# Staging keys and queries in two full PSUM banks, the last query chunk's maxima from one block-diagonal operand, and a fourth split step per head

## The chip, the cores and the metric

The kernel runs on one core of a Trainium2 chip. TensorE (PE in the rows; its weight loads are PEld) multiplies matrices into PSUM, VectorE (DVE) and ScalarE (ACT) read PSUM and write on-chip memory, GpSimd (POOL) works on on-chip memory alone, and SyncE (SP) issues the DMAs. Each engine runs its own instructions in order. The metric is device time per execution in microseconds (us), the median of several executions. Before the change it is 1091.69 us (three runs, 1090.48 to 1095.55).

## What is computed

Three layers follow each other, all in float32. The first is attention over 4 batches of 8 heads, with 576 queries (each the mean of two rows of q) and 1152 keys of 64 elements:

```
q_pool = q.reshape(B, H, S // 2, 2, D).mean(axis=3)
scores = scale * q_pool @ k^T
attn   = softmax(scores);  out = attn @ v
```

The second is a mixture of four causal attention heads over 576 tokens of 512 features, of which two per token count. The third mixes each token with the one before it, and multiplies a sigmoid gate with the product of a squared ReLU layer of 1024 and a second matrix.

## The kernel before

A float32 number goes through TensorE in one of two ways. Either a matmul takes the float32 operand as it is ("native", line 786; a native matmul is two records in the trace), or the number is split into a rounded high part and the rest, both of a faster type, and products of the parts are summed: high by high, high by low, low by high (lines 793 to 795). A copy with rounding makes the high part, a subtraction the low part (`dve_lo`, line 145).

The first layer runs head after head, 32 of them (`hh`), each in nine steps (`s1_job`). A step takes two 128-key chunks of one half of the queries (288 of them). It makes two tiles of scores with two matmuls each: KA by QA (line 758) and KB by QB (line 759). KA holds the keys' high parts twice (in partitions 0 to 63 and 64 to 127), QA the queries' high and low parts; KB holds the keys' low parts and a row of ones, QB the queries' high parts and, in row 64, the negative maximum of each query, so that the exponential (ACT, line 766) needs nothing more. A step then is `n` (native: the exponentials p multiply the float32 values in VF) or `sv` (ACT copies the high part ph, line 64, and DVE subtracts, line 71, giving pl). In heads 2 to 31, steps 0, 3 and 6 are native, the other six are split. The product with the values follows four steps later.

Beside the steps runs the work for later heads, as tasks that are spread over a stretch of steps:

- `s1_prep(hh+2)`, from three steps before the start of head `hh` to one step after it. POOL adds the pairs of query rows; TensorE transposes the keys (line 635, four transposes into one PSUM bank, a fifth into a second) and the queries (line 681, three into a third bank). The keys are copied and subtracted into a staging tile `sk` (high and low), of which there is one buffer; the copies are ACT's in batch 0 and DVE's after it (`kh0`, `kh1`). The queries go straight from PSUM into QA (two copies by ACT, two subtractions by DVE, each 64 by 288). Two steps later in the program, SP issues six DMAs from `sk` to KA and KB (lines 670 to 672) and two from QA to QB (line 711).
- `s1_max(hh+1)`, from 4.5 steps before the start of head `hh` to at least 4.5 steps after it (somewhat later in heads 0 to 2): for each of five query chunks (four of 128, the last of 64) three matmuls of 384 keys (line 728), each with a DVE maximum over the 384 (line 730). `max_finish` turns the result by a transpose (line 402), and one DMA writes the row of QB (line 404).

In batches 1 to 3 the second layer's work of the batch before is merged between the steps of heads 0 to 6 (queries and keys, line 348; its attention, lines 467 to 496; its output, line 548). Heads 2 to 8, 15 and 23 have none of it: nine plain steps.

All instructions of the first two layers are written in program order and then placed on the engines by a scheduler; TensorE is the exception, whose order is the written one. Four PSUM banks ("bank") serve transposes, maxima and sums of values alike, two pairs of banks ("st") the scores.

Of the kernel before, what the change touches and what calls it, by code (L numbers as in the profile page):

```python
# [55 lines left out]
def tile_kernel(ctx: ExitStack, tc: tile.TileContext, q, k, v, w_gate, wq, wk, wv, wo,  # L56
# [112 lines left out]
    def drive(steps, tasks, drain=False):  # L169
# [4 lines left out]
        for i, st in enumerate(steps):  # L174
# [219 lines left out]
    def max_finish(PMs, QB, name):  # L394
# [176 lines left out]
    EK = -(-NC // 2) * P  # L571
# [16 lines left out]
    raw = {}  # L588
# [23 lines left out]
    def s1_prep(hh):  # L612
# [16 lines left out]
        def tk(c0, c1):  # L629
            def f():  # L630
# [6 lines left out]
                e0 = c0 // 2 * P  # L637
                if kst:
                    hi, lo_ = (sk[:m, j, e0 : e0 + w] for j in range(2))
                    copy(kh, hi, ps[:m, :w])  # L640
                    dve_lo(lo_, ps[:m, :w], hi)
                else:
                    for up in range(m // D):
                        a, cs = own[up], slice(e0 + up * EK, e0 + up * EK + w)
                        copy(kh, KAi[a, cs], ps[a, :w])
                        if first:
                            act_hi(KAi[own[1 - up], cs], ps[a, :w])
                    for up in range(m // D):
                        a, cs = own[up], slice(e0 + up * EK, e0 + up * EK + w)
                        los.append((KBi[0:D, cs], ps[a, :w], KAi[a, cs]))  # L650
                    if not first:
                        lo()
                if c1 == NC and not first:
                    later(G["dup"], dup_k)
# [7 lines left out]

        halves = (slice(0, EK), slice(EK, S))

        def dup_k():
            for up in range(2):
                a, z, cs = own[up], own[1 - up], halves[up]
                w = cs.stop - cs.start
                if kst:
                    nc.sync.dma_start(f32(KAi[a, cs]), f32(sk[a, 0, :w]))  # L670
                    nc.sync.dma_start(f32(KAi[z, cs]), f32(sk[a, 0, :w]))
                    nc.sync.dma_start(f32(KBi[0:D, cs]), f32(sk[a, 1, :w]))
                else:
                    nc.sync.dma_start(f32(KAi[z, cs]), f32(KAi[a, cs]))
# [3 lines left out]
        def tq():  # L678
            ps = aux()
            for t in range(NQ // 2):  # L680
                nc.tensor.transpose(ps[:, t * QW : (t + 1) * QW], qp[:, 2 * t * D : (2 * t + 2) * D], ident[:QW, :QW])  # L681
            qq.append(ps)
            if qst:
                copy(G["qh" + ("0" if hh < H else "1")], sq[:, 0], ps[:, :HT])
                dve_lo(sq[:, 1], ps[:, :HT], sq[:, 0])
            else:
# [617 lines left out]
```

## Time and profile before

| | |
|---|---|
| median of 3 runs | 1091.69 us |
| profiled execution | 1094.68 us, of which the span of the core's instructions is 1092.3 us |
| mean granted TensorE clock | 0.986 of full |
| TensorE busy | 1024.0 us (94%) |
| TensorE weight loads | 884.7 us (81%) |
| DVE busy | 826.6 us (76%) |
| ACT busy | 583.8 us (53%) |

The profiled execution took 3.0 us more than the median. The heads of the first layer fill the span from 7.5 us to about 739 us (first and last matmul of line 758). Busy times overlap: a matmul's record lasts 0.29 us while the next one starts 0.13 us after it, so a busy share of TensorE is more than the share in which columns flow.

### The profile page before, as it was taken

To read this page: it belongs to the slowest core of one execution; us is meant where nothing else is said; L and a number is where in the kernel's file an instruction comes from. 1 tells how busy PE (TensorE), PEld (TensorE's weight loads), DVE (VectorE), ACT (ScalarE), POOL (GpSimd) and SP (SyncE) were. 2 spreads that over 40 slices of the span, in tenths; PEclk is the share of its full clock that TensorE was granted. 3 is DMA by queue.
4 is the path that set the end of the run, shared out by engine and by line. 5 is a ranking of instruction groups with operands and counts; after the bars stand their busy time and mean duration, and the time that the engine had idled before them with its cause. 6 is when DMAs were issued, how large, how long until landed. Compare 5 with 4: busy or idle time off the path is not lost. (4 is left out here: it accounts for less than half of the span.)

```text
span 1092.3 us, 18217 instructions
## 1 busy us (share of the span) xinstructions
PE 1024.0 (94%) x6480; PEld 884.7 (81%) x6480; DVE 826.6 (76%) x1753; ACT 583.8 (53%) x1011; POOL 187.8 (17%) x277
## 2 busy tenths in 40 slices
PE   5999999998999999999999999988888799999998
PEld 3888888887887887787788888878876688888887
DVE  5899999789899889799989988876776634444442
ACT  4667777557576556666656666663454312222222
POOL 6341111011111102021201111021012001111110
PEclk9999999999999999999999999999898899999999
DMA  5656545344543544544454453147245311111100
GB/s 123 147 136 158 128 117 141 101 116 111 132 132 93 161 117 116 147 124 113 107 170 127 98 140 85 38 148 233 98 163 154 112 44 39 40 39 39 39 21 19
DMA packets 129095, 119.23 MB, mean 109 GB/s; under 512 B 63751, under 2 KB 91358, under 8 KB 129006
## 3 DMA queue, kind: packets, MB, share of 16 engines
q1 hardware_dynamic: 129006, 118.08, 40.4%
q8 instruction: 51, 0.84, 0.3%
q14 instruction: 38, 0.31, 0.1%
HBM read 63.24 MB, written 20.07 MB: 76 GB/s over the span
## 5 line engine op out<-in xcount | busy, mean ns | idle before, releaser
L730 DVE TENSOR_REDUCE PM<-bank 128x1 f32<-128x384 f32 (+1 forms) x480 | 254.3, 546 | 27.3 <-PE bank L728 23.6
L766 ACT ACTIVATE p<-st 128x576 f32<-128x576 f32 x288 | 186.4, 649 | 117.0 <-PE st L759 113.2
L728 PE MATMUL bank<-KA,QA 128*128 128x384 f32 (+1 forms) x480 | 187.0, 398 | 15.6 <-DVE KB L145 4.3
L758 PE MATMUL st<-QA,KA 128*128 128x288 f32 x576 | 176.7, 320 | 3.4 <-ACT p L766 2.9
L759 PE MATMUL st<-QB,KB 65*128 65x288 f32 x576 | 163.9, 299 | 0.0
L71 DVE TENSOR_TENSOR pl<-p,ph 128x576 fp32r<-128x576 f32 x190 | 148.3, 781 | 13.1 <-ACT ph L64 11.1
L64 ACT ACTIVATE ph<-p 128x576 fp32r<-128x576 f32 x190 | 130.2, 685 | 17.1 <-PE bank L794 7.3
L758 PEld LDWEIGHTS st<-QA,KA 128*128 128x128 f32 x576 | 110.5, 192 | 13.3 <-ACT p L766 4.0
L793 PE MATMUL bank<-ph,VV 128*65 128x288 f32 x384 | 117.5, 306 | 1.9 <-DVE sk L145 0.9
L728 PEld LDWEIGHTS bank<-KA,QA 128*128 128x128 f32 (+1 forms) x480 | 87.9, 185 | 36.4 <-DVE PM L730 8.1
L786 PE MATMUL bank<-p,VF 128*65 128x288 f32 x384 | 114.6, 409 | 0.7 <-DVE PM L409 0.6
L795 PE MATMUL bank<-pl,VV 128*65 128x288 f32 x384 | 113.2, 295 | 0.0
L794 PE MATMUL bank<-ph,VV 128*64 128x288 f32 x384 | 112.9, 294 | 0.0
L759 PEld LDWEIGHTS st<-QB,KB 65*128 65x128 f32 x576 | 110.5, 192 | 2.4
L1101 PE MATMUL sth<-xkh,wk 128*128 128x256 f32 x512 | 91.4, 279 | 1.2 <-ACT relu L1108 1.2
L1108 ACT ACTIVATE relu<-sth 128x512 f32<-128x512 f32 x32 | 17.5, 596 | 122.4 <-PE sth L1101 121.6
L1101 PEld LDWEIGHTS sth<-xkh,wk 128*128 128x128 f32 x512 | 78.7, 188 | 1.8 <-ACT relu L1108 1.4
L71 POOL TENSOR_TENSOR VV<-VF,VV 128x576 fp32r<-128x576 f32 x32 | 44.7, 1396 | 200.2 <-ACT VV L64 175.0
L625 POOL TENSOR_TENSOR qp<-qr 96x384 f32<-96x384 f32 x31 | 34.5, 1113 | 217.1 <-PE bank L681 162.7
L1101 PE MATMUL sth<-xkl,wk 128*128 128x256 f32 x256 | 71.4, 279 | 0.0
L786 PEld LDWEIGHTS bank<-p,VF 128*65 128x65 f32 x384 | 51.9, 139 | 20.4 <-DVE PM L409 1.2
L482 POOL TENSOR_SCALAR_AFFINE_SELECT p<-p 128x128 f32<-128x128 f32 (+1 forms) x96 | 34.4, 388 | 196.5 <-ACT p L474 196.4
(205 smaller groups left out, 2235.5 us busy)
## 6 DMA issues: line engine op xcount, KB each, us to landing
KA<-sk SPq DMA_DIRECT2D x60, 160.0 KB
qr<-in_q_dram SPq DMA_DIRECT2D x32, 288.0 KB
kr<-in_k_dram SPq DMA_DIRECT2D x32, 288.0 KB
VF<-in_v_dram SPq DMA_DIRECT2D x32, 288.0 KB
KA<-sk SPq DMA_DIRECT2D x60, 128.0 KB
R<-scr SPq DMA_DIRECT2D x48, 144.0 KB
w3h<-w3st SPq DMA_DIRECT2D x20, 256.0 KB
w3l<-w3st SPq DMA_DIRECT2D x20, 256.0 KB
```

Source lines behind the costliest of these rows:

```text
L64: nc.scalar.activation(dst, src, AF.Copy)
L71: eng[e].tensor_tensor(dst, src, hi.bitcast(F32), op=ALU.subtract)
L728: nc.tensor.matmul(ps[:n, : 3 * P], QA[i][:, t0 : t0 + n], KA[i][:, 3 * g * P : 3 * (g + 1) * P], start=True, stop=True)
L730: nc.vector.tensor_reduce(pm[:n, c, g : g + 1], ps[:n, : 3 * P], axis=AX.X, op=ALU.max)
L758: nc.tensor.matmul(st[:, n, :HT], KA[i][:, ks], QA[i][:, cs], start=True, stop=False)
L759: nc.tensor.matmul(st[:, n, :HT], KB[i][0 : D + 1, ks], QB[i][0 : D + 1, cs], start=False, stop=True)
L766: nc.scalar.activation(pt, st[:, :, :HT], AF.Exp, scale=1.0 / 16.0)
L786: nc.tensor.matmul(a[: D + 1, :HT], VF[hh % NF][:, c], cell["p"][:, n], start=c == 0, stop=c == NC - 1)
L793: nc.tensor.matmul(a[: D + 1, :HT], vh, ph[:, n], start=c == 0, stop=False)
L794: nc.tensor.matmul(a[:D, :HT], vl, ph[:, n], start=False, stop=False)
L795: nc.tensor.matmul(a[: D + 1, :HT], vh, pl[:, n], start=False, stop=c == NC - 1)
L1101: nc.tensor.matmul(st[:, f // 2, f % 2 * GT : (f % 2 + 1) * GT], w[kt][:, fs], x[:, kt], start=i == 0, stop=i == 3 * KT - 1)
```

## The change

1. **Split steps.** In heads 2 to 31 step 3 turns from native into split; two native steps (0 and 6) are left.
2. **Staging.** The tile `sk` becomes wider (640 key columns and 288 query columns, high and low). The first bank of keys is staged as before. A second bank takes one more transpose of the keys (the last two chunks together) and the three transposes of the queries, and one copy and one subtraction of 416 columns on all 128 partitions move it into `sk`. So the fifth key transpose's own copy and subtraction and the four 64 by 288 operations on the queries go. The copies are ACT's in all heads (`kh1` is `s`). QA and QB are now filled from `sk` by six DMAs, where two were. The order of the key columns in KA changes with the layout (`kcol`).
3. **Maxima of the last 64 queries.** Two DMAs write the last 64 queries' high parts into a block-diagonal operand `BD`: partitions 0 to 63 with columns 0 to 63, partitions 64 to 127 with columns 64 to 127. One matmul of BD with the 512 first columns of `sk` gives the scores of these queries against the even chunks in rows 0 to 63 and against the odd chunks in rows 64 to 127; a second one with 128 columns gives chunk 8 (and chunk 7 once more). Two maxima (512 and 128 columns) stand where three of 384 stood. A small minimum joins the two halves of the row (negative maxima), and the row of QB is written by two DMAs.
4. **TensorE's order at the start.** The first steps of head 0, up to three before head 1, are driven outside the manual order, so that the scheduler places TensorE's instructions there too.

The core of the diff; of the table G, which is one line, only the two entries for the split steps and one for the copies differ:

```diff
-'S0': ('n', 'sv', 'sv', 'n', 'sv', 'sv', 'n', 'sv', 'sv')
+'S0': ('n', 'sv', 'sv', 'sv', 'sv', 'sv', 'n', 'sv', 'sv')
-'S1': ('n', 'sv', 'sv', 'n', 'sv', 'sv', 'n', 'sv', 'sv')
+'S1': ('n', 'sv', 'sv', 'sv', 'sv', 'sv', 'n', 'sv', 'sv')
-'kh1': 'v'
+'kh1': 's'
...
-            nc.sync.dma_start(f32(QB[D : D + 1, 0 : 5 * P]).rearrange("o (a c) -> o a c", a=5), f32(mr))
+            if not halves:
+                nc.sync.dma_start(f32(QB[D : D + 1, 0 : 5 * P]).rearrange("o (a c) -> o a c", a=5), f32(mr))
+                return
+            n = T % P
+            low = sm.tile([5, n], F32R, tag="ml", name=f"ml{name}")
+            nc.vector.tensor_tensor(low, f32(mr[:, :n]), f32(mr[:, n:]), op=ALU.min)
+            nc.sync.dma_start(f32(QB[D : D + 1, 0 : 4 * P]).rearrange("o (a c) -> o a c", a=4), f32(mr[0:4]))
+            nc.sync.dma_start(f32(QB[D : D + 1, 4 * P : T]), f32(low[4:5]))
...
-    EK = -(-NC // 2) * P
+    EK = NC // 2 * P
+    SW = EK + P
...
+        sk = None if first else s1a.tile([P, 2, SW + HT], F32R, tag="sk", name=f"sk{hh}")
...
+        def stage(ps, c, w):
+            copy(kh, sk[:, 0, c : c + w], ps[:, :w])
+            dve_lo(sk[:, 1, c : c + w], ps[:, :w], sk[:, 0, c : c + w])
...
+        def tkq():
+            ps = aux()
+            qq.append(ps)
+            nc.tensor.transpose(ps[:, :P], kr[:, (NC - 2) * D : NC * D], ident)
+            tq(P)
+            stage(ps, EK, P + HT)
+            later(G["dup"], dup_q)
+            later(G["dup"], dup_k)
...
-                    nc.sync.dma_start(f32(QBi[0:D, cs]), f32(QAi[a, cs]))
+                nc.sync.dma_start(f32(QAi[a, cs]), f32(sk[a, 0, SW:]))
+                nc.sync.dma_start(f32(QAi[z, cs]), f32(sk[a, 1, SW:]))
+                nc.sync.dma_start(f32(QBi[0:D, cs]), f32(sk[a, 0, SW:]))
+            n = T % P
+            for up in range(2):
+                nc.sync.dma_start(f32(BD[hh % 2][own[up], up * D : up * D + n]), f32(sk[own[1], 0, SW + HT - n :]))
...
+        def half(g):
+            c0, w = ((0, EK), (EK, P))[g]
+
+            def f():
+                if hh < 4 and g == 0:
+                    nc.vector.memset(pm[:, len(TC) - 1, 2:3], -3.0e38)
+                ps = aux()
+                nc.tensor.matmul(ps[:, :w], BD[hh % 2], staged[hh][:, 0, c0 : c0 + w], start=True, stop=True)
+                nc.vector.tensor_reduce(pm[:, len(TC) - 1, g : g + 1], ps[:, :w], axis=AX.X, op=ALU.max)
+            return f
+
+        if hh >= G["nf1"]:
+            return [half(0), half(1)] + some(0, len(TC) - 1) + [lambda: max_finish(pm, QB[i], f"1_{hh}", True)]
...
+    free = at_[1][0] - 3
+    drive(steps[:free], tasks)
     with tc.manual_schedule(engines={mybir.EngineType.PE}):
-        drive(steps, tasks, drain=True)
+        drive(steps[free:], tasks, drain=True, first=free)
```

How the instructions stand, at three places. The first is TensorE around the start of head 6, a head of plain steps: the staging transposes of head 8 and the first maximum of head 8. In the names, `st_6_0` is the score tile of head 6, step 0; `kr` and `qp` are the raw keys and pooled queries; `p` and `ph` the exponentials. Before:

```order
L635 MATMUL bank_1773<-ident,kr_1602 64x128
...
L758 MATMUL st_6_0_1789<-QA_177,KA_175 128x288
L759 MATMUL st_6_0_1789<-QB_178,KB_176 128x288
...
L728 MATMUL bank_1797<-KA_179,QA_181 128x384
L681 MATMUL bank_1800<-ident,qp_1725 128x96 x3
...
L759 MATMUL st_6_4_1898<-QB_178,KB_176 128x288
L786 MATMUL bank_1910<-p_6_0_1794,VF_185 65x288
L728 MATMUL bank_1912<-KA_171,QA_173 128x384
```

And in the changed kernel:

```order
L735 MATMUL bank_1826<-KA_179,QA_181 128x384
L699 MATMUL bank_1829<-ident,kr_1632 128x128
L685 MATMUL bank_1829<-ident,qp_1765 128x96 x3
L778 MATMUL st_6_0_1836<-QA_177,KA_175 128x288
L779 MATMUL st_6_0_1836<-QB_178,KB_176 128x288
...
L779 MATMUL st_6_4_1943<-QB_178,KB_176 128x288
L806 MATMUL bank_1955<-p_6_0_1841,VF_185 65x288
L750 MATMUL bank_1957<-sk_1766,BD_198 128x512
```

The query transposes moved from behind the scores of step 0 to ahead of them, into the bank of the last key transpose, and the first maximum of head 8 (line 750), at the same place as before, now reads `sk` and BD in the place of KA and QA. Between the staging transposes and that maximum lie five steps' scores, six maxima of 384 columns, 18 matmuls of split steps and three native ones (of two records each).

The second place is SP's queue for the same staging of head 8 (`sk_1726` before, `sk_1766` in the changed kernel). Before:

```order
L255 DMA R_4_1661<-scr_4_1660 64x576
L670 DMA KA_171<-sk_1726 64x512
L597 DMA kr_1834<-in_k_dram 128x576
L671 DMA KA_171<-sk_1726 64x512
L670 DMA KA_171<-sk_1726 64x640
L671 DMA KA_171<-sk_1726 64x640
L672 DMA KB_172<-sk_1726 64x640
L672 DMA KB_172<-sk_1726 64x512
L711 DMA QB_174<-QA_173 64x288 x2
L602 DMA VF_186<-in_v_dram 128x9x64
```

And in the changed kernel (the left-out rows are the same three of the second half of the queries, and the rest of the keys):

```order
L675 DMA KA_171<-sk_1766 64x512
L255 DMA R_4_1697<-scr_4_1696 64x576
L612 DMA kr_1873<-in_k_dram 128x576
L715 DMA QA_173<-sk_1766 64x288
L716 DMA QA_173<-sk_1766 64x288
L717 DMA QB_174<-sk_1766 64x288
...
L720 DMA BD_198<-sk_1766 64x64 x2
L676 DMA KA_171<-sk_1766 64x512
L677 DMA KB_172<-sk_1766 64x512
...
L617 DMA VF_186<-in_v_dram 128x9x64
```

Ahead of BD's two DMAs stand six for the queries, of which the second (line 716) reads the low part; five of the six DMAs for the keys come behind BD.

The third place is the start: SP's rows from the keys of head 2 to the row of maxima of head 1 (`mr_1`). Before:

```order
L672 DMA KB_172<-sk_366 64x640
L597 DMA kr_489<-in_k_dram 128x576
L711 DMA QB_174<-QA_173 64x288 x2
L596 DMA qr_657<-in_q_dram 96x6x128
L404 DMA QB_182<-mr_1_499 1x5x128
```

And in the changed kernel:

```order
L716 DMA QA_173<-sk_368 64x288
...
L720 DMA BD_198<-sk_368 64x64 x2
L677 DMA KB_172<-sk_368 64x512
L675 DMA KA_171<-sk_368 64x640
L676 DMA KA_171<-sk_368 64x640
L677 DMA KB_172<-sk_368 64x640
L405 DMA QB_182<-mr_1_502 1x5x128
```

The row for head 1 (line 405) stands behind all of head 2's staging DMAs, ten of them from the first that reads the queries' low part.

## Rows read from the trace of the kernel before

**Rows 1.** The page's busy times: us, share of the span, instructions.

```profile
PE 1024.0 (94%) x6480; PEld 884.7 (81%) x6480; DVE 826.6 (76%) x1753; ACT 583.8 (53%) x1011; POOL 187.8 (17%) x277
```

**Rows 2.** Busy times by stretch: us from the start, its length, each engine, granted clock.

```profile
core 0: us, PE busy (x) PEld busy (x) DVE busy (x) ACT busy (x) POOL busy (x), PEclk, DMA share, GB/s
61.00:181.00 120.00, 116.31 (x758) 100.19 (x756) 113.44 (x224) 87.98 (x151) 22.36 (x20) 1.00 0.57 137
255.00:338.00 83.00, 77.28 (x499) 66.10 (x498) 74.12 (x170) 52.23 (x91) 13.69 (x22) 0.98 0.44 115
331.00:335.00 4.00, 4.00 (x18) 3.74 (x19) 3.13 (x7) 1.58 (x3) 0.78 (x3) 0.60 0.02 5
454.00:537.00 83.00, 77.22 (x501) 66.00 (x500) 74.42 (x170) 53.56 (x94) 13.85 (x23) 0.98 0.43 112
631.00:724.00 93.00, 91.69 (x610) 79.30 (x609) 75.80 (x175) 62.36 (x108) 11.73 (x21) 1.00 0.36 86
```

**Rows 3.** TensorE's timeline in head 0: start, us, line, output and inputs.

```profile
39.76 1.13 PE L786 MATMUL bank<-p,VF 128*65 128x288 f32 x4
40.52 0.51 PE L758 MATMUL st<-QA,KA 128*128 128x288 f32 x1
...
41.26 0.34 PE L728 MATMUL bank<-KA,QA 128*128 128x384 f32 x1
41.44 0.29 PE L793 MATMUL bank<-ph,VV 128*65 128x288 f32 x1
41.57 0.29 PE L794 MATMUL bank<-ph,VV 128*64 128x288 f32 x1
```

**Rows 4.** Groups by shape: count, busy us, mean ns, idle before and its releaser.

```profile
L71 DVE TENSOR_TENSOR pl<-p,ph 128x576 fp32r<-128x576 f32 x190 | 148.3, 781 | 13.1 <-ACT ph L64 11.1 <-PE st L759 0.6
L64 ACT ACTIVATE ph<-p 128x576 fp32r<-128x576 f32 x190 | 130.2, 685 | 17.1 <-PE bank L794 7.3 <-ACT U L134 3.1 <-DVE sk L66 1.1
...
L730 DVE TENSOR_REDUCE PM<-bank 64x1 f32<-64x384 f32 x96 | 51.1, 540 | 6.1 <-PE bank L728 5.5
...
L145 DVE TENSOR_TENSOR QA<-bank,QA 64x288 fp32r<-64x288 f32 x64 | 29.1, 454 | 5.9 <-ACT QA L64 4.6
...
L64 ACT ACTIVATE QA<-bank 64x288 fp32r<-64x288 f32 x63 | 25.3, 402 | 5.3 <-PE bank L681 4.4
...
L145 DVE TENSOR_TENSOR sk<-bank,sk 128x512 fp32r<-128x512 f32 x30 | 20.4, 681 | 0.4 <-ACT sk L64 0.3
...
L66 DVE CAST sk<-bank 128x512 fp32r<-128x512 f32 x24 | 16.3, 678 | 0.5 <-PE bank L635 0.5
```

**Rows 5.** Instructions on the staging tile: count, duration ns least/median/most, first and last start.

```profile
L145 DVE TENSOR_TENSOR sk<-bank,sk x60: 269/477/692, 31.0 to 676.9; 128x512 fp32r<-128x512 f32 x30, 64x128 fp32r<-64x128 f32 x30
...
L672 SPq DMA_DIRECT2D KB<-sk x60: 461/554/1587, 32.2 to 680.3; - x60
...
L64 ACT ACTIVATE sk<-bank x12: 254/420/599, 30.4 to 113.7; 128x512 fp32r<-128x512 f32 x6, 64x128 fp32r<-64x128 f32 x6
```

**Rows 6.** The same view of the tile of maxima: a maximum over 512 columns.

```profile
L428 DVE TENSOR_REDUCE PM<-bank x16: 667/672/678, 221.6 to 816.0; 64x1 f32<-64x512 f32 x16
```

**Rows 7.** Waits of TensorE, 61 to 724 us: total us, times, longest.

```profile
PE bank L728 <- DVE PM L730: 3.2, 7, 1.2
```

**Rows 8.** SP's timeline around the start of head 6: start, us.

```profile
127.34 0.50 SPq L251 DMA_DIRECT2D scr<-rd  x1
129.04 0.47 SPq L255 DMA_DIRECT2D R<-scr  x1
...
134.79 1.57 SPq L711 DMA_DIRECT2D QB<-QA  x2
```

**Rows 9.** TensorE's timeline in head 5: the query transposes of head 7.

```profile
115.10 0.41 PE L681 MATMUL bank<-ident,qp 96*128 96x96 f32 x3
```

**Rows 10.** DVE's timeline there: the low parts of the same queries.

```profile
117.28 0.92 DVE L145 TENSOR_TENSOR QA<-bank,QA 64x288 fp32r<-64x288 f32 x2
```

**Rows 11.** SP's timeline at the start: the row of maxima of head 1.

```profile
38.40 0.85 SPq L404 DMA_DIRECT2D QB<-mr  x1
```

**Rows 12.** TensorE's timeline: the first scores of head 1.

```profile
43.46 0.30 PE L758 MATMUL st<-QA,KA 128*128 128x288 f32 x1
```

More of the change, by code (lines that the diff above doesn't have):

```diff
@@ L167, in tile_kernel, with drive @@
     lagged = []
-    def drive(steps, tasks, drain=False):
+    def drive(steps, tasks, drain=False, first=0):
         def fill(t):
@@ L172, in fill @@
                 x.run(t)
-        for i, st in enumerate(steps):
+        for i, st in enumerate(steps, first):
             now[0] += 1
@@ L586, in tile_kernel, with kcol @@
         nc.vector.memset(PM[i], 0.0)
-    raw = {}
+    BD = [s1.tile([P, P], F32R, name=f"BD{i}") for i in range(2)]
+    for i in range(2):
+        nc.gpsimd.memset(f32(BD[i]), 0.0)
+    raw, staged = {}, {}
+    def kcol(c):
+        return 2 * EK if c == NC - 1 else c // 2 * P + c % 2 * EK
     def s1_load(hh):
@@ L616, in s1_prep @@
         own = (slice(0, D), slice(D, P))
-        kst, qst = (G["kst"] and not first, G["qst"] and not first)
         KAi, KBi, QAi, QBi = KA[i], KB[i], QA[i], QB[i]
         qp = s1a.tile([QW, NQ * D], F32, tag="qp", name=f"qp{hh}")
-        sk = s1a.tile([P, 2, EK], F32R, tag="sk", name=f"sk{hh}") if kst else None
-        sq = s1a.tile([P, 2, HT], F32R, tag="sq", name=f"sq{hh}") if qst else None
+        sk = None if first else s1a.tile([P, 2, SW + HT], F32R, tag="sk", name=f"sk{hh}")
+        staged[hh] = sk
         kh = G["kh" + ("0" if hh < H else "1")] if hh else "s"
@@ L636, in f @@
                     w += P
[L637 to L654, printed above, removed]
+                if not first:
+                    stage(ps, 0, w)
+                    return
+                cols = [(own[up], own[1 - up], slice(kcol(c0 + up), kcol(c0 + up) + w)) for up in range(m // D)]
+                for a, z, cs in cols:
+                    copy(kh, KAi[a, cs], ps[a, :w])
+                    act_hi(KAi[z, cs], ps[a, :w])
+                for a, z, cs in cols:
+                    los.append((KBi[0:D, cs], ps[a, :w], KAi[a, cs]))
             return f
@@ L676, in s1_prep, with tq @@
-        qhalf = (slice(0, HT), slice(HT, T))
-        def tq():
+            for up, cs in enumerate((slice(0, EK), slice(EK, S))):
+                a, z, w = own[up], own[1 - up], cs.stop - cs.start
+                nc.sync.dma_start(f32(KAi[a, cs]), f32(sk[a, 0, :w]))
+                nc.sync.dma_start(f32(KAi[z, cs]), f32(sk[a, 0, :w]))
+                nc.sync.dma_start(f32(KBi[0:D, cs]), f32(sk[a, 1, :w]))
+        qhalf = (slice(0, HT), slice(HT, T))
+        def tq(w0=0):
+            ps = qq[-1] if w0 else aux()
+            for t in range(NQ // 2):
+                c = w0 + t * QW
+                nc.tensor.transpose(ps[:, c : c + QW], qp[:, 2 * t * D : (2 * t + 2) * D], ident[:QW, :QW])
+            if w0:
+                return
+            qq.append(ps)
+            for up in range(2):
+                a, cs = own[up], qhalf[up]
+                copy(G["qh" + ("0" if hh < H else "1")] if hh else "sv"[up], QAi[a, cs], ps[a, :HT])
+            for up in range(2):
+                a, z, cs = own[up], own[1 - up], qhalf[up]
+                dve_lo(QAi[z, cs], ps[a, :HT], QAi[a, cs])
@@ L679, in tq @@
+        def tkq():
             ps = aux()
-            for t in range(NQ // 2):
-                nc.tensor.transpose(ps[:, t * QW : (t + 1) * QW], qp[:, 2 * t * D : (2 * t + 2) * D], ident[:QW, :QW])
             qq.append(ps)
[L683 to L686, printed above, removed]
-                for up in range(2):
-                    a, cs = own[up], qhalf[up]
-                    copy(G["qh" + ("0" if hh < H else "1")] if hh else "sv"[up], QAi[a, cs], ps[a, :HT])
-                for up in range(2):
-                    a, z, cs = own[up], own[1 - up], qhalf[up]
-                    dve_lo(QAi[z, cs], ps[a, :HT], QAi[a, cs])
@@ L693, in tq @@
-            if not first:
-                later(G["dup"], dup_q)
+            nc.tensor.transpose(ps[:, :P], kr[:, (NC - 2) * D : NC * D], ident)
[3 more added lines that the diff above has]
+            later(G["dup"], dup_k)
         qq = []
@@ L755, in qk @@
                 for n, (j, c) in enumerate(items):
[L756 removed]
+                    cs, k0 = slice(j * HT, (j + 1) * HT), kcol(c)
                     ks = slice(k0, k0 + P)
```

24 lines of the change are left out of this document (4 added, 20 removed).

## The prediction, made before the changed kernel ran

> **What bounds the kernel now.** I read the busy times of the page first [rows 1]: TensorE stands at 94% and DVE at 76%, ACT at 53%. An average over unlike heads doesn't say which of the two ends a head, so I cut the span by heads next [rows 2]. The reader is to see three kinds. The 120 us from 61 are seven plain heads of 17.1 us each: TensorE 116.3, DVE 113.4 (95%). The two stretches of 83 us are three heads each (12 to 14, 20 to 22) with much of the second layer: TensorE 93%, DVE 89 to 90%, clock 0.98. I count 11 such heavy heads (10, 12 to 14, 17, 18, 20 to 22, 25, 26). The 93 us from 631 (heads 27 to 30) stand for the ten others, light for DVE: TensorE 98.6%, DVE 82%. So in light heads TensorE alone sets the time; in plain ones both are nearly full; in heavy ones TensorE has gaps while DVE is close to full.
>
> The timeline of TensorE [rows 3] says what a busy share is worth: split matmuls of 288 columns last 0.29 us but start 0.13 apart (41.44, 41.57), a maximum of 384 holds the next one back by 0.18 (41.26 to 41.44). So the columns need less than the record's time, and the gaps inside are real, though small.
>
> **TensorE's part.** A native step has two products, four records from 39.76. The next matmul begins at 40.52 and lasts 0.51 where one of its size lasts 0.29, so its columns flow from 40.74: 0.98 us for two products, 0.49 each [rows 3]. A split product is three matmuls of 0.13, 0.39. The change turns two per head: 2 x 0.10 = 0.20 us less. A chunk's three maxima are 3 x 0.18 = 0.54; instead come 512 columns (0.18 x 512/384 = 0.24) and 128 (0.06 by columns, 0.13 if it goes like one of 288; I take 0.10): 0.20 less. The transposes are as many as before. Together 0.40 us per head, 12 us in 30 heads.
>
> **DVE's part** [rows 4 to 6]. Per head there go three maxima of 384 on the last chunk (3 x 0.540), two low parts of the queries (2 x 0.454) and the low part of 128 keys (0.28; the 60 low parts of `sk` lie at 0.269 to 0.692, half of them that small): 2.81. In the 24 heads of batches 1 to 3 the two copies, 0.678 and about 0.27, go as well: 3.76. There come one pl (0.781), a low part of 416 columns (between 0.454 at 288 and 0.681 at 512; 0.58), a maximum of 512 (0.672), one of 128 (0.28, as for the small low part) and a small minimum (0 to 0.27; 0.20): 2.51. Net 0.30 less in 6 heads, 1.25 less in 24: 31.8 us.
>
> ACT pays for it: in batches 1 to 3 one ph (0.685), a copy of 512 (0.42 to 0.60) and of 416 (about 0.51) come, two of 0.402 go: +1.0 per head, some 25 us in all. In heavy heads ACT is busy 52 to 54 of 83 us [rows 2], so that hides; were it late, the score tiles would come free later, at most its 1.0 per head.
>
> **What a microsecond of DVE is worth.** In heavy heads I take 1.1 of 1.25 us: DVE reads the banks that TensorE waits for, and the stretch has 5.7 us without TensorE records in 83, 1.9 per head. But the waits named for that in 660 us are small: three maxima account for 3.2 us in 7 waits, at most 1.2 [rows 7]. So the low end is TensorE's own 0.40, the high one 1.25. 11 x 1.1 = 12.1 us (4 to 14). In light heads TensorE's 0.40 counts: 4.0 us (0 to 12, if DVE's part counts there too).
>
> The Trainium skill, page "Perfetto Trace Analysis", section "Identifying the Most-Contended Engine", holds that matmul busy time judges TensorE badly, that its weight-load share is the better measure, and that the engine with the highest occupancy is the one to improve first. By that DVE, 113.4 against 100.2 us of weight loads in the plain heads and 74.1 against 66.1 in the heavy ones [rows 2], would be the bound, and its whole cut would be the gain: rival B below. The trace agrees in so far as records overlap (0.29 against 0.13), and disagrees in the light heads, where DVE has 17 us idle in 93.
>
> **The new chain to BD.** The maxima of head hh+2's last chunk used to read KA and QA; now they need `sk` and BD, and BD comes by DMA behind six others on SP. In a plain head the staging transposes and the first of these maxima stand where they stood, with this between them: 20 score matmuls (2.6 us), six maxima (1.08), 18 split matmuls (2.36), three native products (1.47): 7.5 us. The chain: landing of a DMA takes some 1.7 us (the row of scr at 127.34, the one that reads it at 129.04), an issue 0.55 us in the median, 0.79 in a pair, 1.59 at worst [rows 5, 8]. From the end of the query transposes (115.10 + 0.41) to their low parts (117.28) pass 1.8 us, plus 0.58 for the new one: 2.35 [rows 9, 10]. Then, counting from the first issue that needs the low part, six issues to the second BD: 6 x 0.554 = 3.3, or 6 x 0.79 = 4.7; then 1.7. That is 7.4 to 8.75 us against 7.5, and 6.2 if the low part comes at once. BD is late by 0 to 1.3 us; I take 0.3. What queues behind that matmul on TensorE is everything: the scores of the next steps, hence ACT and DVE. Plain heads: 9 x (-0.40 + 0.3) = -0.9 us (-3.6 to +9). In heavy and light heads the second layer's matmuls widen the 7.5 us, and I put the wait at nothing. The six of `sk`'s DMAs that the next head's copies wait for have a whole head's time. SP issues seven more DMAs per head, 4 us of 17: hidden otherwise.
>
> **Start.** Head 1's row of maxima was issued at 38.40 and head 1's scores began at 43.46 [rows 11, 12]. It now stands behind ten DMAs after head 2's low part: 10 x 0.55 = 5.5 us, of which part was there before (eight then), and with the landing and the row's own issue I get 43.6 to 46.2 for the scores, against 43.46. The first steps of head 0, which the scheduler may now place between tasks, can lose or gain about as much. I take +2.5 (-2 to +6).
>
> **Clock.** At 331 to 335 the granted clock is 0.60 in the mean, so for most of it the lower level of 1.2 GHz; 0.98 over each 83 us is 1.7 us lost each [rows 2]. TensorE had idled before it. With a shorter DVE some such dips go: -2 us (-5, all of them and two alike, to +3, new ones behind BD).
>
> **Sum** against the profiled execution, 1094.68: -12.1 - 4.0 - 0.9 + 2.5 - 2 = -16.5, 1078.2. The runs' median is 3.0 lower: 1075 us, 1.5% less.
>
> **Rivals.**
> A is the forecast, 1075, by its terms' bounds 1066 to 1086: chance 0.55.
> B: DVE sets the pace everywhere, since each PSUM bank comes free only when DVE has read it. For it: 95% and 89% in plain and heavy heads. Against: the light heads, and the small named waits. Then all 31.8 us go: 1060. Chance 0.13.
> C: nothing much comes. In heavy heads the banks turn by the latency from engine to engine, not by DVE's load, so only 0.40 x 11 = 4 us go; light heads 2, plain heads +2, start +4, clock 0: 1092. For it: the small waits of [rows 7]; against: DVE at 89%, where a later arrival queues. Chance 0.18.
> D, slower: the queue of SP. If the issues that follow the low part take 1.0 us each (between the median 0.55 and the worst 1.59), BD comes at 2.35 + 6.0 + 1.7 = 10.0 us, 2.5 late, in nine plain heads: +22.5, start +4.5; against it -12.1 - 4.0 - 3.6. That is +7.3: 1099. It cancels the gain from 1.7 us of wait per plain head on, and is slower by over 0.5% from 2.3. For it: five of seven issues new and in one row; against: the median. Chance 0.14.
> That the change doesn't do what it says I exclude: the order shows both maxima on BD, and the split steps.
>
> **How the numbers follow.** A measurement of this kernel can tell about 0.5%, 5.5 us, from no change, so below 1086.2 is faster and above 1097.2 slower. Faster: 0.52 of A, all of B, 0.03 of C: 0.68. Same: 0.03 of A, 0.14 of C, 0.03 of D: 0.20. Slower: 0.01 of C, 0.11 of D: 0.12. The range goes from B's 1060 to 1094, so that half of B and most of D, under 0.2, are outside. A's own range is 1066 to 1086.
>
> **What would show it.** DVE's busy time near 795 us, ACT's near 609. Heavy stretches shorter by 3 x 1.1 us, light ones by 0.4 per head, plain ones by nearly nothing. Waits of TensorE on a DMA into BD of at most 0.3 us per plain head (2.5 would be D). Head 1's first scores near 46 us. Clock above 0.98 in the heavy stretches. I am wrong if DVE's share falls in heavy heads and their length doesn't (C), or if light and plain heads shrink by over 1 us each (B).

## The result, and the profile of the changed kernel

The changed kernel takes 1103.71 us (median of five runs, 1101.27 to 1111.82); the kernel before has a median of 1094.2 us over five runs, the three earlier ones included. The ratio, which weighs all the runs and not the medians alone (their quotient is 1.0087), is 1.0107, 95% interval 1.0062 to 1.0152: 1.1% slower, where 1.5% faster was forecast. The profiled execution, 1111.82 us, is the slowest of the five. It is 17 us longer than the profiled one of the kernel before, where the medians differ by 9.5, so its waits and its low clock stand for somewhat more than the median's loss.

The page's busy times, which answer to [rows 1]:

```profile
PE 1021.6 (92%) x6510; PEld 895.8 (81%) x6510; DVE 803.3 (72%) x1677; ACT 597.1 (54%) x1029; POOL 189.2 (17%) x279
```

DVE lost work as intended, and its share fell with no gain. So I cut the span as before, by heads, now from the first exponential of a head. Heads 0 and 1, heads 2 to 31, the plain heads 5 to 7, the heavy ones 12 to 14 and the light ones 27 to 30, changed kernel (columns as in [rows 2]):

```profile
18.90:69.30 50.40, 41.23 (x219) 33.57 (x218) 34.42 (x74) 26.90 (x49) 15.77 (x17) 0.86 0.49 112
69.30:751.90 682.60, 639.78 (x4287) 566.14 (x4285) 570.45 (x1225) 451.34 (x784) 109.84 (x144) 0.98 0.56 136
125.40:177.80 52.40, 48.71 (x328) 43.18 (x327) 44.68 (x88) 38.16 (x66) 6.90 (x6) 1.00 0.62 138
266.30:349.20 82.90, 75.90 (x499) 65.34 (x498) 72.66 (x164) 54.72 (x96) 12.03 (x23) 0.98 0.54 136
647.30:741.60 94.30, 91.70 (x626) 80.88 (x624) 75.85 (x172) 64.57 (x111) 16.37 (x28) 1.00 0.44 105
```

The same cuts in the kernel before:

```profile
62.30:739.20 676.90, 646.85 (x4259) 559.81 (x4258) 595.21 (x1303) 436.95 (x763) 106.45 (x142) 0.99 0.48 123
115.10:166.00 50.90, 49.63 (x326) 42.94 (x325) 49.06 (x98) 36.92 (x63) 7.23 (x6) 1.00 0.53 129
255.80:338.50 82.70, 76.98 (x496) 65.64 (x494) 74.34 (x171) 51.57 (x91) 14.19 (x23) 0.98 0.45 116
631.40:728.70 97.30, 93.78 (x625) 81.14 (x623) 77.91 (x177) 63.30 (x109) 14.91 (x28) 1.00 0.39 99
19.00:62.30 43.30, 38.17 (x219) 31.43 (x219) 35.18 (x76) 27.66 (x54) 17.59 (x19) 1.00 0.51 123
```

Length less TensorE's busy time is the time without a matmul. In heads 2 to 31 that was 676.9 - 646.9 = 30.0 us and is now 682.6 - 639.8 = 42.8. TensorE has 7 us less to do, and waits 13 more. Of these stretches only the light one got shorter (94.3 for 97.3); the plain one went from 50.9 to 52.4, with DVE down from 96% to 85%. Cut head by head in the same way, the eleven heavy heads took 3.3 us more in all, the nine plain ones 2.9 more and the ten light ones 0.5 less; heads 16, 21 and 24 alone took 4 to 5 us more each. The first two heads took 7.1 us more. What follows the first layer is untouched by the change; it took 358 us in this execution, 353 in the one of before.

Part of what remains is a slower clock. These are five of the seven stretches at the lower level (0.50, 1.2 GHz) in the changed kernel's first layer:

```profile
96.40:99.80 3.40, 3.35 (x12) 2.56 (x13) 1.47 (x4) 0.41 (x1) 0.00 (x0) 0.50 0.93 202
28.10:34.90 6.80, 6.27 (x20) 4.93 (x20) 5.88 (x13) 3.71 (x7) 2.84 (x4) 0.50 0.42 106
45.20:52.00 6.80, 6.23 (x24) 4.64 (x23) 3.44 (x7) 1.93 (x3) 0.00 (x0) 0.50 0.75 167
372.90:379.70 6.80, 6.56 (x25) 6.03 (x26) 2.07 (x3) 0.88 (x3) 0.00 (x0) 0.50 0.66 159
512.80:519.60 6.80, 6.63 (x30) 6.23 (x30) 3.96 (x10) 1.72 (x3) 0.70 (x3) 0.50 0.17 61
```

At half speed they cost 30.6 / 2 = 15.3 us; with the other two, of 3.4 us each (at 321.7 and 574.3), it is 18.7 us. In its first layer the kernel before had three such stretches of 3.4 us (one in [rows 2]), 5.1 us lost. In the changed kernel TensorE had stood still for 1.3 to 3.7 us shortly before each of them. Its longest totals of waits from 60 to 760 us, changed kernel:

```profile
PE st L476 <- DMA QB<-mr: 6.3, 5, 2.1
PE sto L556 <- ACT YH L64: 6.0, 2, 3.4
PE bank L750 <- DMA BD<-sk: 4.5, 2, 3.7
```

(YH is the high part of the second layer's normalised output; line 476 multiplies its scores, line 556 its output.)

The longest, 3.7 us, is in head 3. Three engines around it (a timeline: start, us; in brackets the idle time before and its releaser), first POOL:

```profile
88.48 1.29 POOL L148 TENSOR_TENSOR wo_l<-wst,wo_h 128x512 fp32r<-128x512 f32 x1
```

then SP:

```profile
86.09 0.53 SPq L612 DMA_DIRECT2D kr<-in_k_dram  x1
89.80 0.33 SPq L876 DMA_DIRECT2D wst<-in_moe_wo_dram  x1
90.22 0.48 SPq L715 DMA_DIRECT2D QA<-sk  x1
...
93.94 1.23 SPq L720 DMA_DIRECT2D BD<-sk  x2
```

and TensorE:

```profile
92.12 0.65 PE L806 MATMUL bank<-p,VF 128*65 128x288 f32 x2
96.45 0.76 PE L750 MATMUL bank<-sk,BD 128*128 128x512 f32 x1 [3.68 <-DMA BD<-sk]
```

The next weights (line 876) go into a tile with one buffer. SP stood at that DMA from 86.62 until POOL had read the old ones at 89.77; then six DMAs of the queries and two of BD followed, the last at 95.17, and TensorE waited until 96.45.

Head 21 shows the other kind: a row of maxima of the second layer. DVE finishes it (`mr`) at 508.07, and SP issues two other DMAs first:

```profile
507.80 0.27 DVE L403 CAST mr<-bank 5x128 fp32r<-5x128 f32 x1
508.23 0.52 SPq L245 DMA_DIRECT2D sd<-U  x1
508.85 0.52 SPq L611 DMA_DIRECT2D qr<-in_q_dram  x1
509.81 0.77 SPq L405 DMA_DIRECT2D QB<-mr  x1
...
512.97 0.58 PE L476 MATMUL st<-QB,KB 65*128 65x288 f32 x1 [2.08 <-DMA QB<-mr]
```

The same row in the kernel before:

```profile
496.72 0.27 DVE L403 CAST mr<-bank 5x128 fp32r<-5x128 f32 x1
497.02 0.76 SPq L404 DMA_DIRECT2D QB<-mr  x1
```

It was issued at once; now it starts 1.7 us after its data, TensorE waits 2.08 us, and the clock is at its lower level from 512.8 to 519.6.

The plain heads show a third kind, and here it is DVE that waits. TensorE waited for BD only once in heads 5 to 7, for 0.8 us. But the sums that normalise a head's output go through three small DMAs on SP (`sd<-U`, `scr<-rd`, `R<-scr`), and DVE stands once per head until `R` is there. Its waits for it in heads 5 to 7, then the rows of heads 5 and 6 (ACT, SP, POOL, DVE):

```profile
DVE XT L835 <- DMA R<-scr: 3.9, 3, 1.8
```

```profile
133.25 0.48 ACT L134 ACTIVATE U<-bank,epsc 65x288 f32<-65x288 f32 x1
134.91 0.53 SPq L245 DMA_DIRECT2D sd<-U  x1
140.95 0.55 SPq L255 DMA_DIRECT2D R<-scr  x1
144.62 1.33 POOL L71 TENSOR_TENSOR VV<-VF,VV 128x576 fp32r<-128x576 f32 x1
145.28 1.28 DVE L835 TENSOR_TENSOR XT<-U,R 64x576 f32<-64x576 f32 x1 [0.93 <-DMA R<-scr]
```

The sums are written at 133.73. SP has issued staging DMAs one after another since 125.94, twelve of them, and comes to the first small one at 134.91, 1.2 us late (0.03 in the kernel before, at 123.35). The product with `R` then falls beside a subtraction of POOL's and takes 1.28 us (1.28 to 1.48 in the three heads, 0.75 in the kernel before). In the kernel before DVE had no such wait in these heads.

### The profile page after: what moved, and what is told of

Read it like the earlier page. It is cut to its first block, busy times and chain, and to the rows that moved or that the text cites. A ratio compares the mean times of both kernels' runs of the same rounds, so it can differ in the third digit from the quotient of the medians.

```text
span 1110.0 us, 18515 instructions
## 1 busy us (share of the span) xinstructions
PE 1021.6 (92%) x6510; PEld 895.8 (81%) x6510; DVE 803.3 (72%) x1677; ACT 597.1 (54%) x1029; POOL 189.2 (17%) x279
## 5 line engine op out<-in xcount | busy, mean ns | idle before, releaser
L737 DVE TENSOR_REDUCE PM<-bank 128x1 f32<-128x384 f32 (+1 forms) x390 | 208.0, 547 | 40.3 <-PE bank L735 38.1
L71 DVE TENSOR_TENSOR pl<-p,ph 128x576 fp32r<-128x576 f32 x220 | 171.5, 780 | 13.4 <-ACT ph L64 11.7
L64 ACT ACTIVATE ph<-p 128x576 fp32r<-128x576 f32 x220 | 150.1, 683 | 33.0 <-PE bank L814 23.7
L735 PE MATMUL bank<-KA,QA 128*128 128x384 f32 (+1 forms) x390 | 152.3, 402 | 12.8 <-DVE KB L145 4.4
L813 PE MATMUL bank<-ph,VV 128*65 128x288 f32 x444 | 134.1, 302 | 1.2 <-DVE sk L145 1.0
L815 PE MATMUL bank<-pl,VV 128*65 128x288 f32 x444 | 132.1, 298 | 0.6 <-DVE pl L71 0.6
L814 PE MATMUL bank<-ph,VV 128*64 128x288 f32 x444 | 131.8, 297 | 0.0
L735 PEld LDWEIGHTS bank<-KA,QA 128*128 128x128 f32 (+1 forms) x390 | 76.6, 198 | 29.1 <-DVE PM L737 6.8
L806 PE MATMUL bank<-p,VF 128*65 128x288 f32 x264 | 83.0, 412 | 0.2
L814 PEld LDWEIGHTS bank<-ph,VV 128*64 128x64 f32 x444 | 60.9, 137 | 8.2 <-issue 0.2
```

Source lines behind the costliest of these rows:

```text
L64: nc.scalar.activation(dst, src, AF.Copy)
L71: eng[e].tensor_tensor(dst, src, hi.bitcast(F32), op=ALU.subtract)
L735: nc.tensor.matmul(ps[:n, : 3 * P], QA[i][:, t0 : t0 + n], KA[i][:, 3 * g * P : 3 * (g + 1) * P], start=True, stop=True)
L737: nc.vector.tensor_reduce(pm[:n, c, g : g + 1], ps[:n, : 3 * P], axis=AX.X, op=ALU.max)
L813: nc.tensor.matmul(a[: D + 1, :HT], vh, ph[:, n], start=c == 0, stop=False)
L814: nc.tensor.matmul(a[:D, :HT], vl, ph[:, n], start=False, stop=False)
```

## Experiments

Each was timed in five rounds beside the kernel before; ratios are to it, with their 95% interval. Four theories run through the expectations: Q, SP's queue; W, the work that was moved costs more than it saves; S, the start alone; P, single stalls from a new placement, with the low clock behind them.

**The split step alone.** The kernel before with `S0` and `S1` of the change:

```diff
-'S0': ('n', 'sv', 'sv', 'n', 'sv', 'sv', 'n', 'sv', 'sv')
+'S0': ('n', 'sv', 'sv', 'sv', 'sv', 'sv', 'n', 'sv', 'sv')   (S1 alike)
```

> The kernel before with only the fourth split step per head. Theory Q (SP's queue is what made the change slower): this part adds no DMA, so its own gain shows, 30 x 0.20 us of TensorE: 1094 - 6 = 1088 us (1085 to 1092). Rival W (the moved work costs more than it saves: ACT copies ph, DVE subtracts pl, and the step waits for both): 1096 us or more. Rival S (the start alone): 1088, like Q.

Measured: 1102.05 us, ratio 1.0096 (1.0061 to 1.0132). Q's number was wrong, and W's held. The kernel's timeline in head 3 (ACT, SP and TensorE):

```profile
83.74 0.35 SPq L872 DMA_DIRECT2D w3st<-in_moe_w_k_dram  x1
...
88.87 0.66 ACT L885 ACTIVATE w3st<-w3st 128x512 f32<-128x512 f32 x1 [6.56 <-DMA kr<-in_k_dram]
89.56 0.65 ACT L766 ACTIVATE p<-st 128x576 f32<-128x576 f32 x1
...
90.26 0.61 PE L758 MATMUL st<-QA,KA 128*128 128x288 f32 x1 [4.43 <-ACT p L766]
```

The scheduler had put the squaring of the third layer's weights (line 885) ahead of an exponential of head 3. It waits 6.56 us for a DMA that was issued at 83.74 (the row names another DMA, the one that came last by the profile), ACT stands, and TensorE waits 4.43 us. That wait is placement and not the split step's price; the next pair separates the two.

**A new placement, without and with the split step.** `blk` holds those weights back until heads 2 and 3 are done:

```diff
-'blk': 1
+'blk': 2
```

> The kernel before with blk 2 alone: the same work, the scheduler places it anew. It measures what a new placement moves by itself. Theory P: anything within +/- 8 us of 1092, and what it moves is in the granted clock and in single waits. Rival W: 1092 +/- 3, since no work is added or removed.

> The kernel before with the fourth split step, and the first two loads of the third layer's weights held back until heads 2 and 3 are finished (the number blk is 2 in the place of 1). Without that, ACT's squaring of those weights stood in front of an exponential of head 3 and kept it 6.6 us. Theory P (the split step itself is cheap; the 1% was the place that the scheduler gave to other work, a stall there, and the low clock after it): the stall in head 3 goes, 1088 to 1096 us. Rival W (the split step's own work on ACT and DVE costs 10 us): 1102 +/- 3.

Measured: `blk` alone 1089.06 us, 1.0000 (0.9980 to 1.0020); with the split step 1091.74 us, 1.0045 (1.0021 to 1.0068), as P had it. So the new placement, without that stall, took away about half of the 10 us. What is left is still a loss, not the 6 us gained that I had put in the sum. Heads 2 to 31 of the second kernel:

```profile
64.20:738.80 674.60, 642.44 (x4319) 561.47 (x4319) 616.84 (x1332) 450.25 (x793) 113.58 (x142) 1.00 0.47 123
```

DVE is busy for 616.8 us where it had 595.2. That pl finds no room there without the new staging is how I read it; the best kernel below, which has the new staging, gains from the same step.

**Six idle DMAs in the kernel before.** Copies of QA that nobody reads, on SP:

```diff
+ nc.sync.dma_start(f32(JK[a]), f32(QAi[a, cs]))
+ nc.sync.dma_start(f32(JK[z]), f32(QAi[a, cs]))        (both for each half)
+ nc.sync.dma_start(f32(JB[own[up], up * D : (up + 1) * D]), f32(QAi[own[1], T - D : T]))   (twice)
```

> The kernel before with six more DMAs per head on SP, of the sizes of the new ones, from QA into tiles that nobody reads. No engine's arithmetic changes. Theory Q: the rows of maxima and the normalisers wait behind them, 1102 to 1115 us, with TensorE waits on them and a granted clock of 0.98 or less. Rival W (work) and rival S (start order): no change, 1094 +/- 3.

Measured: 1132.23 us, ratio 1.0379 (1.0337 to 1.0420), beyond even Q's range. Heads 2 to 31, and TensorE's largest total of waits from 60 to 790 us:

```profile
63.00:781.80 718.80, 667.36 (x4259) 574.83 (x4258) 596.03 (x1303) 436.21 (x763) 108.35 (x147) 0.96 0.52 129
```

```profile
PE st L468 <- DMA QB<-mr: 6.5, 6, 3.8
```

DVE and ACT have the same work as before; 51.4 us are without a matmul (30.0 before), and the clock is 0.96. The placement of all else is new here too, so not all of the 41 us need be the DMAs' own.

**The changed kernel with three native steps**, and **with the old maxima** (no BD, the `sk` staging kept):

> The changed kernel with three native steps as before (only the split part undone). Rival W (the split step's work costs 10 us, as it did alone): 1094 us. Theory Q and P (SP's queue, and single stalls with the low clock after them): the waits on BD at 44 and 93 us stay, 1100 to 1108 us.

> The changed kernel with the maxima of the last 64 queries as before (three of 384 from KA and QA, one row DMA), so without BD; staging and split steps stay. Three DMAs per head fewer on SP, 0.75 us more DVE per head. Theory Q: part of the loss goes, 1095 to 1100 us, and no wait on BD. Rival W: DVE's extra 0.75 us per head shows, 1104 to 1120. Rival S: about 1100 (the wait of 3.2 us on BD at 44 us goes).

Measured: 1105.64 us, 1.0152 (1.0123 to 1.0181), and 1100.55 us, 1.0092 (1.0058 to 1.0127). Neither differs clearly from the change (1.0107), so neither part alone brings the loss. The first is as Q and P had it and rules W out for the split step. The second lies just above Q's range and is also what S had; but its first two heads last 50.1 us, as in the change (50.4), so S's reason for it does not hold. Without BD TensorE waits for KA instead (8.0 us in five waits): the queue is as late for the next one in it.

**The new DMAs on another queue.** QA's four DMAs and BD's two are issued by GpSimd:

```diff
- nc.sync.dma_start(f32(QAi[a, cs]), ...)      (four into QA, two into BD)
+ nc.gpsimd.dma_start(f32(QAi[a, cs]), ...)
```

> The changed kernel with the six new DMAs per head (four into QA, two into BD) issued by GpSimd's queue in the place of SP's. TensorE's order is the same. Theory Q: 1080 to 1092 us, the waits on BD shorter. Rival W: 1104 +/- 3, as the work of DVE and ACT is the same. Rival S: 1098 to 1101, only the start is relieved.

Measured: 1093.76 us, 1.0022 (0.9999 to 1.0045): some 10 us better than the change, just outside Q's range, and its waits on BD did not get shorter (from 30 to 740 us):

```profile
PE bank L750 <- DMA BD<-sk: 13.3, 5, 6.6
```

In the change the same row is 7.7 us in three waits. So TensorE waits more for BD and the kernel is faster all the same: BD's lateness is not the main loss. In head 3 GpSimd issues BD's two last, at 94.66, behind its own work on the weights and QA's four, and TensorE has them at 100.86. So BD's two went back to SP, ahead of all, and QA's four stayed on GpSimd:

> The changed kernel with BD's two DMAs first on SP and the four DMAs into QA issued by GpSimd. Theory Q: BD is written some 4 us earlier than with all of them on one queue, the waits on BD shrink from 13 us (all six on GpSimd) to 4 or less, and with the low clock after them 1082 to 1092 us. Rival W: 1094, no gain over the kernel with all six on GpSimd.

Measured: 1067.51 us, ratio 0.9803 (0.9772 to 0.9833): 2% faster than the kernel before, with all the work of the change, and better than Q had it. I call it the best kernel from here on. Its heads 2 to 31, and heads 5 to 7, 12 to 14, 27 to 30:

```profile
65.00:710.30 645.30, 626.21 (x4287) 556.43 (x4286) 565.69 (x1228) 450.01 (x785) 165.85 (x256) 1.00 0.55 143
114.90:161.90 47.00, 47.00 (x329) 43.42 (x328) 45.72 (x91) 37.91 (x66) 14.44 (x19) 1.00 0.66 165
248.50:327.40 78.90, 75.27 (x503) 64.49 (x502) 71.95 (x164) 54.21 (x95) 22.09 (x37) 1.00 0.52 135
606.70:700.00 93.30, 91.61 (x626) 80.73 (x624) 75.77 (x172) 64.75 (x112) 21.18 (x40) 1.00 0.42 105
```

Plain heads take 15.7 us where they took 17.0 (17.5 in the change), and TensorE has no gap in them, nor DVE a wait for `R`; 19.1 us of the 645.3 are without a matmul, and the clock is full. Three variants show what did it, BD's place or QA's queue, and that it isn't one lucky placement:

> The changed kernel with BD's two DMAs ahead of the queries' six, all on SP: only the order in the queue changes. Theory Q1 (it is BD's place in the queue): most of the 36 us between the changed kernel and x_mix come, 1068 to 1080. Theory Q2 (it is the length of the queue: normalisers and rows of maxima wait behind it, heads 16, 21 and 24): the waits on BD at 44, 93 and 150 us go and the others stay, 1085 to 1097.

> The changed kernel with only QA's four DMAs on GpSimd; BD's two stay behind QB's two on SP. Theory Q1 (taking four DMAs off SP is what matters, BD then stands only two issues later): 1066 to 1075 us. Theory Q2 (BD must be ahead of all that needs the low parts): 1080 to 1092.

> The kernel x_mix with blk 2: the third layer's weights start a head later and the scheduler places everything anew, with the same DMAs on the same queues. Theory Q (which queue holds which DMA decides): 1064 to 1073 us, as x_mix. Rival L (x_mix owes its time to one lucky placement): 1078 us or more.

BD first but all on SP, as Q2 had it: 1089.46 us, 1.0016 (0.9995 to 1.0037). QA on GpSimd and BD where the change had it: 1073.18 us, 0.9804 (0.9779 to 0.9829). The best one with `blk` 2, all placed anew: 1073.36 us, 0.9789 (0.9757 to 0.9821); by the time it is 0.4 us above Q's range, by the ratio it is as good as the best one, since the kernel before took 1095.1 us beside these two. QA's queue alone gives the best kernel's ratio, so taking the four DMAs off SP is what matters; BD's place is worth some 0.9% as long as all are on SP (1.0107 to 1.0016), and nothing once they aren't. Plain heads 5 to 7 of the kernel with BD first still show SP's hand. TensorE has no wait for BD there, DVE has the one for `R`:

```profile
118.90:169.80 50.90, 48.48 (x329) 43.31 (x328) 45.38 (x88) 38.23 (x66) 6.88 (x6) 1.00 0.64 143
```

```profile
DVE XT L835 <- DMA R<-scr: 3.5, 3, 1.4
```

These heads last 3.9 us longer than the best kernel's. One thing the move does not separate: QA's four leave SP's issue order and also go by another DMA queue (q0 of the profile beside q1), so how much of the gain is issue time and how much transfers that no longer stand behind them was not tried.

**The split step where nothing is late, and the start.** The best kernel with three native steps, and with the manual order from the first step:

> The kernel x_mix (BD first on SP, QA's four DMAs on GpSimd) with three native steps per head in the place of two. It weighs the split step where nothing waits for SP's queue. Theory P (a split step is worth its 0.20 us of TensorE per head once TensorE has no gaps): 1067.5 + 6 = 1073 us (1071 to 1077). Rival W (the split step's work on ACT and DVE costs more than it saves, as in the kernel before with blk 2, +5 us): 1060 to 1065.

> The kernel x_mix with TensorE's manual order from the start of head 0, as before the change. Theory: the free order moved several scores of head 0 ahead of the transposes of head 1, so the maxima of head 1 wait and the clock falls at 28.6 us; without it head 1 begins some 2 us earlier at the full clock: 1062 to 1066. Rival (the free order gains what it loses): 1067.5 +/- 2. Against the kernel before at 1088 to 1092.

Measured: 1081.33 us, 0.9935 (0.9911 to 0.9958), and 1067.28 us, 0.9807 (0.9776 to 0.9839). Here the split step is worth 1.3%, about 14 us, more than either theory had (P: 6). Not all of that need be the step's own: in the profile of the kernel with three native steps TensorE waits 3.2 us once for a sum of values (U), with 3.4 us of low clock behind it, as a new placement can bring. The free order at the start gains what it loses, as the rival said.

**QB's two DMAs off SP as well**, on GpSimd, then on ACT:

> The kernel x_mix with QB's two DMAs on GpSimd too: GpSimd issues six DMAs per head, SP two fewer. Theory Q (the length of SP's queue still costs): the normalisers come earlier, 1060 to 1066 us. Rival (SP's queue is no longer late, and GpSimd issues at 0.5 us each in order between its own work, so QB comes later): 1068 to 1078 us.

> The kernel x_mix with QB's two DMAs issued by ACT, which wrote their source itself. SP is as short as in the kernel with six DMAs on GpSimd (1093 us), GpSimd as light as in x_mix. Theory G (GpSimd's six DMAs make its own subtractions fall beside DVE's and delay DVE): 1062 to 1072 us. Rival R (QB, or the rows behind it, comes later once it leaves SP): 1080 to 1095.

Measured: 1093.04 us, 1.0013 (0.9996 to 1.0030), and 1085.44 us, 0.9900 (0.9865 to 0.9935). Both are slower than the best one, the first by more than its rival had, the second as rival R had it, so a shorter queue is not better by itself. One wait of DVE, here from 60 to 700 us, is longer in both; first the best kernel:

```profile
DVE rd L248 <- DMA sd<-U: 8.4, 8, 2.4
```

then with QB on GpSimd, and on ACT:

```profile
DVE rd L248 <- DMA sd<-U: 19.6, 16, 2.6
```

```profile
DVE rd L248 <- DMA sd<-U: 15.4, 15, 2.5
```

The reciprocal of a normaliser stands in DVE's order before its data is there, and the maxima behind it keep their banks: TensorE's waits for them at the key transposes (line 649) come to 8.4 us with QB on GpSimd and 4.8 with QB on ACT (44 to 760 us), and to none in the best kernel. With QB on GpSimd one more thing is seen, here in head 6:

```profile
136.23 1.00 POOL L639 TENSOR_TENSOR qp<-qr 96x384 f32<-96x384 f32 x1 [4.88 <-PE bank L685]
136.25 1.60 DVE L71 TENSOR_TENSOR pl<-p,ph 128x576 fp32r<-128x576 f32 x1
...
139.20 0.74 DVE L71 TENSOR_TENSOR pl<-p,ph 128x576 fp32r<-128x576 f32 x1
```

The same subtraction takes 1.60 us beside one of GpSimd's and 0.74 alone. GpSimd issues no QB in the kernel with QB on ACT, which lies halfway between; how much of the 26 us is which of the two was not tried.

## Why the prediction was wrong

1. **The step that failed** is the sentence "SP issues seven more DMAs per head, 4 us of 17: hidden otherwise", with the one shortly before it that put the wait at nothing in heavy and light heads. The price was right: SP's rows in heads 5 to 7 add up to some 30 us of issuing before and 41.5 after, 4 us more per head. The one chain that was worked out was right in size too: TensorE waited 0.8 us for BD in three plain heads, 0.3 per head forecast. What was wrong is "hidden": past the start, nothing was set for what stands behind these DMAs on SP. That is the sums in plain heads (DVE stood 1.3 us per head for `R`), the rows of maxima (6.3 us of TensorE's waits from 60 to 760 us, 0.2 before) and, it seems, the second layer's sums: TensorE's waits for YH, which needs their `R`, rose from 0.7 to 6.0 us in heads 16 and 24, though in head 16 SP issued that `R` only 0.7 us later after the DMA ahead of it in the chain than before (3.5 us, 2.8). Behind the longest of these waits came the low clock. Heavy, light and plain heads came out at +3.3, -0.5 and +2.9 us where -12.1, -4.0 and -0.9 stood in the sum. Six idle DMAs in the kernel before cost it 3.8%; four of the new ones on another queue turn the change from 1.1% slower to 2% faster.
2. **Clock.** I forecast 2 us back. It took 18.7 us instead of 5.1 in the first layer: in the changed kernel all six waits of TensorE of over 2 us there were followed by a stretch at 1.2 GHz. The difference, 13.6 us, is more than the 12.7 us by which the first layer grew between the two profiled executions. The sign followed from step 1: once the waits are gone (the best kernel) the clock stays at 1.00 in heads 2 to 31.
3. **Start.** Head 1's first scores came at 47.0, near the 46 that was forecast and within the term's bounds. But the start lost more before head 2: its first exponential is at 69.3 instead of 62.3, +7.0. The queue was seen (ten DMAs ahead of head 1's row); the wait on BD there (3.2 us) and two stretches of low clock, 6.8 us lost, were not. The first of the two also stands in the best kernel (28.6 to 35.4) and not with the manual order, so it comes with the free order, and not with SP; since both kernels take as long, that loss is made up elsewhere.
4. **TensorE's part was about right.** Busy time less what the low clock stretched: 646.9 - 5.1 before, 639.8 - 11.9 after (the 18.7 us lost in all less the start's 6.8): 13.9 us less, 12 forecast.
5. **DVE's and ACT's parts were right by their parts.** The summed durations of DVE's named instructions fall by 31 us (QA 27, copies 23, maxima 20 less; pl 23, the wider low part 9, the minimum 6 more), 31.8 forecast. Others became longer, the product with `R` by 4.5 us in all, and the page shows 23. ACT's rise by 24 us (ph 20, staging copies 28 more; QA 24 less), 25 forecast; the page, where records overlap, shows 13.
6. **What a microsecond of DVE is worth** can be read from the best kernel, where nothing is late on SP. Its heavy heads lost 12.8 us in all (12.1 forecast, though here part of it is the clock). For plain heads it was set too low: I gave them TensorE's 0.40 alone, and heads 5 to 7 lost 1.3 us each, about DVE's whole cut of 1.25. There the rule of the Trainium skill ("Perfetto Trace Analysis", "Identifying the Most-Contended Engine"), to improve the engine of highest occupancy first, holds: DVE at 96% was that engine, against 84% of weight loads. In the light heads 27 to 30 it isn't (80% against 83%), and still 1.0 us per head came where TensorE's 0.40 was forecast.
7. **Rivals.** D named the right engine, SP, and the wrong place: its 2.5 us of wait on BD per plain head came nowhere near (0.8 us in three heads; what these heads show instead is DVE's wait for `R`). Its chance of 0.14 was too low, since I counted SP's share of time (4 us of 17) and not that it works in order. The forecast's gain was there: the best kernel, 1067.5 us, lies between A and B. Two small slips moved nothing: 9 x (1.3 - 0.4) is 8.1, not 9, and the 6.2 us for a low part that comes at once would be 5.6 to 7.0 by its own terms.

What stays open: why moving QB off SP costs 1 to 2%, beyond the reciprocal's wait and the slower subtractions; how much of the 41 us of the six idle DMAs is placement; and whether SP's issuing or the transfers of its queue held the rows back.

## What to carry to other kernels

A queue that issues in order can be an engine on the path, however small the share that a change adds: for each added DMA list what stands behind it, and ask for each of these who waits and for how long. Look at every engine's waits for DMAs, not TensorE's alone: in the plain heads DVE was the one that stood. Try bulky transfers on another queue than the small rows that are needed at once, and measure each move: four of six paid here, BD's two and QB's two on GpSimd did not. Test one part of a change alone only beside a re-placed kernel without it, since here one weight conversion in the wrong place cost about as much as the part itself.

## What the runs showed of the hardware

- In the first layer of the changed kernel each of six waits of TensorE of 2.1 to 3.7 us was followed by 3.4 or 6.8 us at 0.50 of the clock, so 1.7 or 3.4 us came on top of the wait. In the kernel before one of 2.2 us was, and two of 2.4 and 2.9 us were not.
- Most issues by SP took 0.5 to 0.6 us (131.64 to 134.80 us of the changed kernel: five in 3.2 us); twelve DMAs in a row held the next one, whose data was there, for 1.2 us.
- A DVE subtraction of 128x576 took 1.60 us beside an addition of GpSimd's, 0.74 us otherwise; a DVE product of 64x576 took 1.28 to 1.48 us beside a subtraction of GpSimd's, 0.75 otherwise.
